# Fourteen gate/up units as 7-product 2x2 blocks, with sums of the down operand on GpSimd

## The chip, the cores and the metric

The kernel runs on one core of one Trainium2 chip. The metric is the device time of one execution in microseconds (us), lower is better. The kernel before takes 265.61 us (median of 20 runs, 265.26 to 267.59).

## The reference, cut to what matters

Two blocks work on 2048 tokens with 640 features, and a sigmoid gate mixes them. Only the second block is touched by the change, except that its down projection is summed with the first block's output projection in one product.

```python
def _B_ref(x, w_gate, w_up, w_down):             # 640 -> 1728 -> 640
    return (_gelu(x @ w_gate) * (x @ w_up)) @ w_down
...
g = _sigmoid((x * gate_w).sum(-1, keepdims=True))
a = _A_ref(x, A_wqkv, A_wo)                      # linear attention
return g * a + (1 - g) * b
```

## The kernel before

The tokens go in four quarters of 512. For each quarter, a *gate/up stage* (13 full f tiles of 128 and one half tile) makes the hidden `hT`; a *down stage* for the previous quarter follows. The order is E(1), down(0), E(2), down(1), E(3), down(2), down(3). An f tile of gate/up is ten matmuls of 512 columns, one gelu on ScalarE and one multiplication on VectorE:

```python
def e_mm(ps, w, ft, q, t0=0, tw=QW):                      # QW = 512, ND = 5
    for dk in range(ND):
        nc.tensor.matmul(ps[:, t0 : t0 + tw], lhsT=w[:, dk, ft * P : (ft + 1) * P],
                         rhs=xT[q][:, dk, t0 : t0 + tw], start=(dk == 0), stop=(dk == ND - 1))

def e_out(q, ft, psg, psu):
    gl = work.tile([P, QW], BF16, name="gl")
    nc.scalar.activation(out=gl[:], in_=psg[:], func=ACT.Gelu_apprx_tanh)
    nc.vector.scalar_tensor_tensor(out=hT_cur[q][:, ft, :], in0=psu[:], scalar=HS, in1=gl[:],
                                   op0=ALU.mult, op1=ALU.mult)
```

Down is already done with 7 instead of 8 products of 2x2 blocks. That needs sums of its first operand over k tiles in three parts: h (6 tiles of `hT`), p (2 tiles of the attention operand `pqT`), x (one mixed tile). Each part has four sums, per half `a` of the tokens, all on VectorE, all with two operands in SBUF:

```python
def phase_S(q, part, a=None):
    ...
    sums(s3, blk(0, 0), blk(1, 0), ALU.subtract)
    sums(s1, blk(1, 0), blk(1, 1), ALU.add)
    sums(s2, s1, blk(0, 0), ALU.subtract)
    sums(s4, blk(0, 1), s2, ALU.subtract)
```

The down stage runs seven products for each half. An accumulator bank `x` is used three times, with a copy by ScalarE (`keep`) between; VectorE joins (`join`). A dictionary says what is queued beside which unit or product ("F": before the first product, "D": behind the first join).

```python
product(x, a, 0, 0, 0, 0, 0, 0, True, True)
c1 = keep("c1", x, 0)                       # ScalarE; product 3 below writes x again
...
product(x, a, 2, 0, 0, 2, 0, 0, False, True)      # product 3, needs c1 done
...
join(d[:], b22, 0, c2)                      # VectorE
beside("D", q, a)
...
(2, 2): [(s_tiles, 1), (phase_S, 1, "h", 0)],     # gate/up stage 2, third unit
(2, 3): [(phase_S, 1, "h", 1)],
(2, 4): [(phase_S, 1, "p"), (phase_S, 1, "x")],
```

Apart from set-up, GpSimd only forms products for the denominators of the attention (`den_mul`, `den_out`).

## Time and profile before

| | before |
|---|---|
| time, median of 20 | 265.61 us |
| span of the profiled run | 264.8 us |
| gate/up stage 2 / down(1) / gate/up 3 / down(2) and (3) | 29.14 / 17.87 / 29.14 / 35.90 us |

The stage lengths here and below are my differences between the starts of first matmuls in the timeline of TensorE; the last one runs to the end of the last matmul.

These are three lines of the page of the kernel before: the busy times of the engines, and the chain that ended last, by engine and by line (L186 is the gate/up matmul, L603 the down matmul).

```profile
PE 258.1 (97%) x1569; PEld 145.0 (55%) x1587; DVE 185.1 (70%) x343; ACT 94.5 (36%) x187; POOL 50.2 (19%) x50
...
PE 93%; DMA 4%; issue 0%; DVE 0%; SPq 0%
PE banks L186 44%; PE banks L603 26%; PE banks L249 14%; PE banks L347 6%; DMA wqk<-in_A_wqkv_dram 3%; PE banks L338 2%; DMA x_all<-in_A_x_dram 1%; PE banks L610 1%; PE banks L478 0%; PE banks L447 0%; DVE o_out L629 0%; SPq L122 0%; PE banks L417 0%
```

TensorE is the bound. The timeline of TensorE gives the price of a unit: start, duration, what, count. The first two lines are the same five matmuls, 1.08 us apart; the last three are the turn from the second to the third product of down(1), without a gap.

```profile
150.18 1.24 PE L186 MATMUL banks<-xT_87,wu 128*128 128x512 bf16 x5
151.26 1.24 PE L186 MATMUL banks<-xT_87,wg 128*128 128x512 bf16 x5
...
179.33 1.11 PE L603 MATMUL banks<-wd,hb 128*128 128x320 bf16 x7
180.28 0.57 PE L603 MATMUL banks<-m_all,pqT_1489 128*128 128x320 bf16 x3
180.68 1.39 PE L603 MATMUL banks<-t_1098,s_2_1578 128*128 128x320 f16 x9
```

The timeline of VectorE in gate/up stage 2 (first fence) has the same sums twice, once while GpSimd works (second fence, the timeline of GpSimd) and once while it rests.

```profile
156.46 1.13 DVE L61 TENSOR_TENSOR sw<-hb 128x768 f16<-128x768 bf16 x1
157.51 1.76 DVE L61 TENSOR_TENSOR s_1_1577<-hb 128x768 f16<-128x768 bf16 x1
...
162.05 0.55 DVE L61 TENSOR_TENSOR sw<-hb 128x768 f16<-128x768 bf16 x1
162.52 0.55 DVE L61 TENSOR_TENSOR s_1_1577<-hb 128x768 f16<-128x768 bf16 x1
```

```profile
154.67 2.50 POOL L533 TENSOR_TENSOR pq_90<-pq_90,rg 128x640 bf16<-128x640 bf16 x2 [2.39 <-DVE rg L524]
157.13 3.40 POOL L510 TENSOR_TENSOR prod<-pq_91,zrep 128x640 f32<-128x640 bf16 x2
```

The same sum takes 0.55 us alone and 1.13 or 1.76 us beside a GpSimd operation. The profile before shows no wait of TensorE in the gate/up and down stages.

### The profile page before, as it was taken

How to read it: one execution, taken by the hardware profiler on the slowest of the kernel's cores; microseconds unless marked ns; L12 is line 12 of the kernel's file. 1: busy time of each engine (PE TensorE's matmuls, PEld its weight loads, DVE VectorE, ACT ScalarE, POOL GpSimd, SP SyncE). 2: the span in 40 equal slices, each digit the busy share in tenths (PEclk: the TensorE clock that was granted, in tenths of full speed). 3: DMA queues.
4: the chain of work that ended last, by engine and by line, in shares of the span. 5: the costliest groups of instructions: out<-in, count | busy, mean ns of one | idle time of the engine just before them, and what ended most of it. 6: DMA issues, size and time to landing. Idle time of an engine off the chain costs nothing.

```text
span 264.8 us, 4162 instructions
## 1 busy us (share of the span) xinstructions
PE 258.1 (97%) x1569; PEld 145.0 (55%) x1587; DVE 185.1 (70%) x343; ACT 94.5 (36%) x187; POOL 50.2 (19%) x50
## 2 busy tenths in 40 slices
PE   8799999999999999999999999999999999999994
PEld 4454444555556775444566544447664444767672
DVE  0765348598889995699994889982335997676132
ACT  3679222655455333832231122223112222312110
POOL 5000000000000003685000762383001820000000
PEclk9999999999999999999999999999999999999999
DMA  7899999000000009125001050022110220011011
GB/s 225 259 285 313 213 321 246 1 0 2 0 0 2 0 16 332 51 59 118 0 0 52 0 136 15 0 54 50 50 50 2 50 50 0 2 50 36 17 50 50
DMA packets 34959, 20.91 MB, mean 79 GB/s; under 512 B 20732, under 2 KB 34940, under 8 KB 34940
## 3 DMA queue, kind: packets, MB, share of 16 engines
q1 hardware_dynamic: 34498, 20.16, 27.8%
q10 hardware_dynamic: 442, 0.49, 0.6%
q8 instruction: 12, 0.20, 0.3%
q14 instruction: 7, 0.06, 0.1%
HBM read 12.62 MB, written 2.62 MB: 58 GB/s over the span
## 4 chain that ended last, share of the span: by engine, by line
PE 93%; DMA 4%; issue 0%; DVE 0%; SPq 0%
PE banks L186 44%; PE banks L603 26%; PE banks L249 14%; PE banks L347 6%; DMA wqk<-in_A_wqkv_dram 3%; PE banks L338 2%; DMA x_all<-in_A_x_dram 1%; PE banks L610 1%; PE banks L478 0%; PE banks L447 0%; DVE o_out L629 0%; SPq L122 0%; PE banks L417 0%
## 5 line engine op out<-in xcount | busy, mean ns | idle before, releaser
L191 ACT ACTIVATE gl<-banks 128x512 bf16<-128x512 f32 x52 | 31.0, 598 | 74.6 <-PE banks L186 70.6
L186 PEld LDWEIGHTS <-wu 128*128 128x128 bf16 x260 | 25.5, 98 | 30.6
L186 PEld LDWEIGHTS <-wg 128*128 128x128 bf16 x260 | 25.2, 98 | 29.3 <-issue 0.5
L192 DVE SCALAR_TENSOR_TENSOR hT_148<-banks,gl 128x512 bf16<-128x512 f32 x26 | 17.4, 682 | 12.7 <-PE banks L186 10.8
L192 DVE SCALAR_TENSOR_TENSOR hb<-banks,gl 128x512 bf16<-128x512 f32 x26 | 17.4, 677 | 10.9 <-PE banks L186 8.7
L266 ACT ACTIVATE phi<-banks 128x512 bf16<-128x512 f32 (+1 forms) x36 | 18.7, 526 | 15.5 <-ACT eneg L267 6.3
L510 POOL TENSOR_TENSOR prod<-pq_89,zrep 128x640 f32<-128x640 bf16 x2 | 2.8, 1406 | 96.2 <-ACT zrep L418 96.2
L625 ACT ACTIVATE m_all<-banks,omg_s 128x320 f32<-128x320 f32 x16 | 8.4, 527 | 27.2 <-PE banks L603 27.2
L629 DVE SCALAR_TENSOR_TENSOR o_out<-banks,omg_s,m_all 128x320 bf16<-128x320 f32 x24 | 12.2, 541 | 5.9 <-PE banks L603 5.9
L186 PE MATMUL banks<-xT_85,wu 128*128 128x512 bf16 x65 | 16.1, 379 | 0.0
L186 PE MATMUL banks<-xT_87,wu 128*128 128x512 bf16 x65 | 16.1, 379 | 0.0
L186 PE MATMUL banks<-xT_88,wu 128*128 128x512 bf16 x65 | 16.1, 379 | 0.0
L186 PE MATMUL banks<-xT_86,wu 128*128 128x512 bf16 x63 | 16.0, 379 | 0.1
L186 PE MATMUL banks<-xT_85,wg 128*128 128x512 bf16 x63 | 16.0, 379 | 0.1
L186 PE MATMUL banks<-xT_87,wg 128*128 128x512 bf16 x62 | 16.0, 379 | 0.2
L186 PE MATMUL banks<-xT_88,wg 128*128 128x512 bf16 x62 | 16.0, 379 | 0.2
L186 PE MATMUL banks<-xT_86,wg 128*128 128x512 bf16 x63 | 15.7, 379 | 0.1
L629 DVE SCALAR_TENSOR_TENSOR m_all<-banks,omg_s,m_all 128x320 f32<-128x320 f32 x8 | 4.4, 551 | 14.6 <-PE banks L603 14.5
L249 PE MATMUL banks<-wqk,xT_85 128*128 128x512 bf16 (+2 forms) x78 | 12.4, 302 | 1.4 <-DMA wqk<-in_A_wqkv_dram 1.3
L510 POOL TENSOR_TENSOR prod<-pq_90,zrep 128x640 f32<-128x640 bf16 x4 | 7.4, 1866 | 24.4 <-DVE den L516 24.4
L629 DVE SCALAR_TENSOR_TENSOR o_out<-banks,omg_s,sw 128x320 bf16<-128x320 f32 x8 | 4.4, 549 | 10.7 <-PE banks L603 5.6
L625 ACT ACTIVATE sw<-banks,omg_s 128x320 f32<-128x320 f32 x8 | 4.2, 527 | 20.6 <-PE banks L603 20.6
(216 smaller groups left out, 469.9 us busy)
## 6 DMA issues: line engine op xcount, KB each, us to landing
out_dram<-o_out SPq DMA_DIRECT2D x16, 160.0 KB, 1.8
wd<-in_B_w_down_dram SPq DMA_DIRECT2D x1, 2080.0 KB
x_all<-in_A_x_dram SPq DMA_DIRECT2D x3, 640.0 KB, 6.2
wqk<-in_A_wqkv_dram SPq DMA_DIRECT2D x1, 800.0 KB
wg<-in_B_w_gate_dram SPq DMA_DIRECT2D x1, 800.0 KB, 8.2
wu<-in_B_w_up_dram SPq DMA_DIRECT2D x1, 800.0 KB
wv<-in_A_wqkv_dram SPq DMA_DIRECT2D x1, 800.0 KB
wo_g<-in_A_wo_dram SPq DMA_DIRECT2D x2, 375.0 KB
```

The lines of the kernel that those rows point to most:

```text
L186: nc.tensor.matmul(ps[:, t0 : t0 + tw], lhsT=w[:, dk, ft * P : (ft + 1) * P], rhs=xT[q][:, dk, t0 : t0 + tw], start=(dk == 0), stop=(dk == ...
L191: nc.scalar.activation(out=gl[:], in_=psg[:], func=ACT.Gelu_apprx_tanh)
L192: nc.vector.scalar_tensor_tensor(out=hT_cur[q][:, ft, :], in0=psu[:], scalar=HS, in1=gl[:], op0=ALU.mult, op1=ALU.mult)
L249: nc.tensor.matmul(ps[:, 0 : hi - lo], lhsT=xT[q][:, dk, sl * P : (sl + 1) * P], rhs=wqk[:, dk, lo:hi], start=(dk == 0), stop=(dk == ND - 1),)
L266: nc.scalar.activation(out=e[:, lo:top], in_=ps[:, lo:top], func=ACT.Exp)
L338: nc.tensor.matmul(gp[:, 0:HALF], lhsT=x_all[:, st, (ND - 1) * P : ND * P], rhs=pk[st][:, j * HALF : (j + 1) * HALF], start=(st == 0), sto ...
L347: nc.tensor.matmul(bank[:, 0:HALF], lhsT=lhsT, rhs=rhs, start=(start and n == 0), stop=(stop and n == NG2 - 1), skip_group_check=True)
L510: nc.gpsimd.tensor_tensor(out=prod[:], in0=pq[st][:], in1=zrep[:], op=ALU.mult)
L603: nc.tensor.matmul(bank[:, 0:HALF], lhsT=lhs(sa, ia, ka * KS + kk, a), rhs=rhs(sb, kb * KS + kk, jb), start=(start and kk == 0), stop=(sto ...
L610: nc.tensor.matmul(bank[:, 0:HALF], lhsT=lhsT, rhs=wd[r : r + FL, NF - 1, j * HALF : (j + 1) * HALF], start=st_, stop=not a, skip_group_ch ...
L625: nc.scalar.activation(out=c[:], in_=bank[:, 0:HALF], func=ACT.Copy, scale=omg[i])
L629: nc.vector.scalar_tensor_tensor(out=out, in0=bank[:, 0:HALF], scalar=omg[i], in1=c[:], op0=ALU.mult, op1=ALU.add)
```

## The change

The intent is to save TensorE time. In gate/up stages 2 and 3, seven of the fourteen units become 2x2 blocks, gate and up by token halves, over four of the five k tiles: one matmul of 512 columns and sixteen of 256 instead of ten of 512. The price is sums of weights (formed once on GpSimd, written out to memory, fetched back a piece per unit), sums of tokens, and a longer evacuation: two accumulator copies and one scaled copy on ScalarE, three VectorE operations, and the final multiplication on GpSimd. To make room on VectorE, the h sums of the first token half go to GpSimd, one at a time, in the slots of the ordinary units between (in quarter 3 one sum of the second half too; nine in all). The core of the diff:

```diff
+    def phase_EW(q, ft, early):
+        ...
+        ew_mm(ub, 1, wt(wu, 4), xt(4, slice(0, QW)), True)
+        ew_mm(ub[:, lo_h], 2, wt(wu, 2), t_(4))
+        ew_mm(gb[:, lo_h], 1, wt(wg, 4), xt(4, lo_h), True)
+        ew_mm(gb[:, hi_h], 1, s_(5), xt(4, hi_h))
+        ew_mm(x[:, lo_h], 2, s_(2), t_(2), False, True)
+        nc.scalar.copy(out=cg[:, hi_h], in_=x[:, lo_h])
+        early()
+        ew_mm(gb[:, lo_h], 2, wt(wg, 2), xt(2, lo_h))
+        ew_mm(ub[:, hi_h], 2, s_(1), t_(1), False, True)
+        ew_mm(gb[:, hi_h], 2, s_(4), xt(2, hi_h), False, True)
+        ew_mm(x[:, lo_h], 2, s_(3), t_(3), False, True)
+        ...
+        nc.vector.tensor_tensor(out=cg[:, hi_h], in0=ub[:, hi_h], in1=cg[:, hi_h], op=ALU.add)
+        nc.scalar.activation(out=ut[:, 1], in_=x[:, lo_h], func=ACT.Copy, scale=HS)
+        ew_finish()                                  # gelu and product of the unit before
+        nc.vector.tensor_tensor(out=cg, in0=gb, in1=cg, op=ALU.add)
+        nc.vector.scalar_tensor_tensor(out=ut[:], in0=ub..., scalar=HS, in1=ut[:, 1:2]..., op0=ALU.mult, op1=ALU.add)
+        def finish():
+            nc.scalar.activation(out=gl[:], in_=cg, func=ACT.Gelu_apprx_tanh)
+            nc.gpsimd.tensor_tensor(out=hT_cur[q][:, ft, :], in0=ut[:]..., in1=gl[:], op=ALU.mult)
...
+    def pool_S(q, a, *which):
+        phase_S(q, "h", a, which, nc.gpsimd)
...
-        (2, 2): [(s_tiles, 1), (phase_S, 1, "h", 0)],
-        (2, 3): [(phase_S, 1, "h", 1)],
-        (2, 4): [(phase_S, 1, "p"), (phase_S, 1, "x")],
...
+        (2, 2): [(pool_S, 1, 0, 3)],
+        (2, 5): [(pool_S, 1, 0, 1), (phase_S, 1, "p", 0, (3, 1))],
+        (2, 8): [(pool_S, 1, 0, 2), (phase_S, 1, "p", 0, (2, 4))],
+        (2, 11): [(pool_S, 1, 0, 4), (phase_S, 1, "x", 0)],
+        (2, 13): [(den_mul, 10, 11)],
+        ("F", 1, 0): [(phase_S, 1, "h", 1), (phase_S, 1, "p", 1), (phase_S, 1, "x", 1)],
...
+        2: [0, 1, 2, -4, -5, 3, -6, -7, 12, -8, -9, 11, -10, 13],     # negative: a new unit
```

The cuts ("...") hide the tiles, the weight sums and the slots of quarter 3, which are like those of quarter 2 but for the down stage, where only three h sums stand before the first product and p and x stand behind the first join.

More of the change, by code (lines that the diff above doesn't have):

```diff
@@ L67 @@
     work = ctx.enter_context(tc.tile_pool(name="work", bufs=3))
+    dram = ctx.enter_context(tc.tile_pool(name="dram", bufs=1, space=bass.MemoryType.DRAM))
     psum = ctx.enter_context(tc.tile_pool(name="psum", bufs=1, space=bass.MemoryType.PSUM))
@@ L89, with pk_tiles @@
     x_sb = [x_all[:, 4 * q : 4 * q + 4, :] for q in range(NQ)]
-    pk_q = [ov.tile([P, 4, D], BF16, name=f"pk{q}", tag="slab_a", bufs=NQ) for q in range(NQ)]
-    pk = [pk_q[t // 4][:, t % 4, :] for t in range(NT)]
+    WF = tuple(range(4, 12))
+    WS = 2 * 4 + 1
+    ws = [ov.tile([P, 2, WS, P], FP16, name=f"ws{i}", tag="slab_a", bufs=NQ) for i in range(3)]
+    ws.append(ov.tile([P, 2, WS, P], FP16, name="ws3", tag="slab_g"))
+    pk_q = []
+    pk = {}
+    def pk_tiles(qs):
+        for q in qs:
+            pk_q.append(ov.tile([P, 4, D], BF16, name=f"pk{q}", tag="slab_a", bufs=NQ))
+            for t in range(4):
+                pk[4 * q + t] = pk_q[q][:, t, :]
+    pk_tiles((0,))
     WQK = 2 * D + 1
@@ L193, in e_out, with phase_E @@
                                        op0=ALU.mult, op1=ALU.mult)
-    def phase_E(q, ft):
+    def phase_E(q, ft, early=None):
         if ft < NF - 1:
@@ L198, in phase_E @@
             e_mm(psg, wg, ft, q)
+            if early:
+                early()
+                ew_finish()
             psu = ps_tile("ps_u")
@@ L204, in phase_E @@
             e_mm(pgu, wgu, 0, q)
+            if early:
+                early()
+                ew_finish()
             gl = work.tile([P, QW], BF16, name="gl")
@@ L208, in phase_E, with w_sums @@
                                            in1=gl[0:FL, :], op0=ALU.mult, op1=ALU.mult)
+    stash = dram.tile([len(WF), P, WS, P], FP16, name="stash")
+    def w_sums(i):
+        f0 = WF[2 * i] * P
+        g, u = (w[:, :, f0 : f0 + 2 * P].rearrange("p k (f c) -> p f k c", f=2) for w in (wg, wu))
+        o = ws[i]
+        s1, s2, s3, s4 = (o[:, :, 2 * n : 2 * n + 2, :] for n in range(4))
+        for out, a0, a1, op in ((s1, u[:, :, 0:2, :], u[:, :, 2:4, :], ALU.add), (s2, s1, g[:, :, 0:2, :], ALU.subtract),
+                                (s3, g[:, :, 0:2, :], u[:, :, 0:2, :], ALU.subtract),
+                                (s4, g[:, :, 2:4, :], s2, ALU.subtract),
+                                (o[:, :, 8:9, :], g[:, :, 4:5, :], u[:, :, 4:5, :], ALU.subtract)):
+            nc.gpsimd.tensor_tensor(out=out, in0=a0, in1=a1, op=op)
@@ new lines, in w_stash, with x_tiles, t_sums, blk @@
+    def w_stash(i):
+        for f in range(2):
+            dma(out=stash[2 * i + f], in_=ws[i][:, f])
+    HT = QW // 2
+    ew = {}
+    def x_tiles():
+        tx = big.tile([P, 4, 2, HT], FP16, name="tx", tag="pq", bufs=NQ)
+        ew["tx"] = [tx[:, n] for n in range(4)]
+    def t_sums(q):
+        def blk(k, j):
+            return xT[q][:, 2 * k : 2 * k + 2, j * HT : (j + 1) * HT]
+        t1, t2, t3, t4 = ew["tx"]
+        for out, a0, a1 in ((t1, blk(0, 1), blk(0, 0)), (t2, blk(1, 1), t1), (t3, blk(1, 1), blk(0, 1)),
+                            (t4, blk(1, 0), t2)):
+            sums(out, a0, a1, ALU.subtract)
@@ new lines, in ew_tiles, with w_fetch @@
+    def ew_tiles():
+        cg = big.tile([P, 2, QW], FP32, name="cg", tag="pq", bufs=NQ)
+        ew["cg"] = [cg[:, 0], cg[:, 1], zacc[:, 0:QW]]
+        ew["n"] = 0
+        ew["first"] = {}
+        ew["open"] = []
+    def w_fetch(*keys, eng=dma):
+        if "ring" not in ew:
+            wr = big.tile([P, 2, WS, P], FP16, name="wr", tag="xT", bufs=NQ - 1)
+            ew["ring"] = [wr[:, 0], wr[:, 1]]
+            ew["m"] = 0
+            ew["at"] = {}
+        for q, ft in keys:
+            slot = ew["ring"][ew["m"] % 2]
+            ew["m"] += 1
+            eng(out=slot, in_=stash[WF.index(ft)])
+            ew["at"][q, ft] = slot
@@ new lines, in ew_finish, with ew_mm, ew_first @@
+    def ew_finish():
+        for f in ew.get("open", ()):
+            f()
+        ew["open"] = []
+    lo_h, hi_h = slice(0, HT), slice(HT, QW)
+    def ew_mm(out, k, lhs, rhs, start=False, stop=False):
+        for n in range(k):
+            nc.tensor.matmul(out, lhsT=lhs(n), rhs=rhs(n), start=start and n == 0, stop=stop and n == k - 1,
+                             skip_group_check=True)
+    def ew_first(q, ft):
+        x = ps_tile("ps_wx")
+        cg = ew["cg"][ew["n"] % 3]
+        ew["n"] += 1
+        ew_mm(x[:, lo_h], 2, lambda n: wg[:, n, ft * P : (ft + 1) * P], lambda n: xT[q][:, n, lo_h], True, True)
+        nc.scalar.copy(out=cg[:, lo_h], in_=x[:, lo_h])
+        ew["first"][q, ft] = x, cg
@@ new lines, in phase_EW, with wt, xt, s_ @@
+    def phase_EW(q, ft, early):
+        fs = slice(ft * P, (ft + 1) * P)
+        sw_ = ew["at"][q, ft]
+        if (q, ft) not in ew["first"]:
+            ew_first(q, ft)
+        x, cg = ew["first"][q, ft]
+        def wt(w, k0):
+            return lambda n: w[:, k0 + n, fs]
+        def xt(k0, c):
+            return lambda n: xT[q][:, k0 + n, c]
+        def s_(i):
+            return lambda n: sw_[:, 2 * (i - 1) + n, :]
+        def t_(i):
+            return lambda n: ew["tx"][i - 1][:, n, :]
+        ub, gb = ps_tile("ps_wu"), ps_tile("ps_wg")
+        ew_mm(ub, 1, wt(wu, 4), xt(4, slice(0, QW)), True)
[4 more added lines that the diff above has]
+        nc.scalar.copy(out=cg[:, hi_h], in_=x[:, lo_h])
+        early()
+        ew_mm(gb[:, lo_h], 2, wt(wg, 2), xt(2, lo_h))
+        ew_mm(ub[:, hi_h], 2, s_(1), t_(1), False, True)
+        ew_mm(gb[:, hi_h], 2, s_(4), xt(2, hi_h), False, True)
+        ew_mm(x[:, lo_h], 2, s_(3), t_(3), False, True)
+        ut = work.tile([P, 2, HT], FP32, name="ut", tag="prod", bufs=2)
+        nc.vector.tensor_tensor(out=cg[:, hi_h], in0=ub[:, hi_h], in1=cg[:, hi_h], op=ALU.add)
+        nc.scalar.activation(out=ut[:, 1], in_=x[:, lo_h], func=ACT.Copy, scale=HS)
+        ew_finish()
+        nc.vector.tensor_tensor(out=cg, in0=gb, in1=cg, op=ALU.add)
+        nc.vector.scalar_tensor_tensor(out=ut[:], in0=ub.rearrange("p (j c) -> p j c", j=2), scalar=HS,
+                                       in1=ut[:, 1:2].to_broadcast([P, 2, HT]), op0=ALU.mult, op1=ALU.add)
+        def finish():
+            gl = work.tile([P, QW], BF16, name="gl")
+            nc.scalar.activation(out=gl[:], in_=cg, func=ACT.Gelu_apprx_tanh)
+            nc.gpsimd.tensor_tensor(out=hT_cur[q][:, ft, :], in0=ut[:].rearrange("p j c -> p (j c)"), in1=gl[:],
+                                    op=ALU.mult)
+        ew["open"].append(finish)
@@ L305, in k_first @@
         held.clear()
-    g_sb = ov.tile([P, ND, D], BF16, name="g_sb", tag="slab_g")
     def x_blk(i, k):
@@ L561, with phase_S @@
     TW = 2 * P
-    def phase_S(q, part, a=None):
+    def phase_S(q, part, a=None, which=(3, 1, 2, 4), eng=nc.vector):
         lo, hi = PART[part]
@@ L568, in blk @@
             return ktiles(part, k, hT_cur[q], pqT[q])[:, :, i * TW + c0 : i * TW + c1]
-        s1, s2, s3, s4 = (SS[q, i][:, lo:hi, c0:c1] for i in range(1, 5))
-        sums(s3, blk(0, 0), blk(1, 0), ALU.subtract)
-        sums(s1, blk(1, 0), blk(1, 1), ALU.add)
-        sums(s2, s1, blk(0, 0), ALU.subtract)
-        sums(s4, blk(0, 1), s2, ALU.subtract)
+        s = {i: SS[q, i][:, lo:hi, c0:c1] for i in range(1, 5)}
+        for i in which:
+            a0, a1, op = {3: (blk(0, 0), blk(1, 0), ALU.subtract), 1: (blk(1, 0), blk(1, 1), ALU.add),
+                          2: (s[1], blk(0, 0), ALU.subtract), 4: (blk(0, 1), s[2], ALU.subtract)}[i]
+            eng.tensor_tensor(out=s[i], in0=a0, in1=a1, op=op)
+    def pool_S(q, a, *which):
+        phase_S(q, "h", a, which, nc.gpsimd)
     side = {}
@@ L681 @@
             phase_E(0, ft)
+            if ft == 5:
+                for i in range(len(ws)):
+                    w_sums(i)
             if ft in (8, 9, 10, 11):
                 x_sums((3, 1, 2, 4)[ft - 8])
+        for i in range(len(ws)):
+            w_stash(i)
+        pk_tiles((1, 2, 3))
+        g_sb = ov.tile([P, ND, D], BF16, name="g_sb", tag="slab_g")
         g4 = [banks[:, b * QW : (b + 1) * QW] for b in (6, 7)]
@@ L743 @@
         (1, 11): [(phase_S, 0, "x", 0)],
-        ("F", 0, 0): [(phase_S, 0, "h", 1)],
+        (1, 12): [(den_mul, 4, 5)],
+        ("F", 0, 0): [(w_fetch, (2, 4), (2, 5)), (phase_S, 0, "h", 1)],
         ("D", 0, 0): [(phase_S, 0, "p", 1), (phase_S, 0, "x", 1)],
-        ("F", 0, 1): [(den_mul, 4, 5)],
-        ("D", 0, 1): [(den_inv, 4), (den_mul, 6, 7), (den_out, 4, 5)],
-        (2, 0): [(den_inv, 6), (den_out, 6, 7)],
-        (2, 2): [(s_tiles, 1), (phase_S, 1, "h", 0)],
-        (2, 3): [(phase_S, 1, "h", 1)],
@@ L751 @@
-        (2, 4): [(phase_S, 1, "p"), (phase_S, 1, "x")],
-        (2, 5): [(den_mul, 8, 9)],
-        (2, 7): [(den_inv, 8), (den_mul, 10, 11), (den_out, 8, 9)],
-        (2, 9): [(den_inv, 10), (den_out, 10, 11)],
-        (3, 0): [(den_mul, 12, 13)],
-        (3, 2): [(den_inv, 12), (den_mul, 14, 15), (den_out, 12, 13)],
-        (3, 4): [(den_inv, 14), (den_out, 14, 15)],
-        (3, 5): [(s_tiles, 2), (phase_S, 2, "h", 0)],
-        (3, 6): [(phase_S, 2, "h", 1)],
-        (3, 7): [(phase_S, 2, "p"), (phase_S, 2, "x")],
@@ L761 @@
-        ("F", 2, 0): [(s_tiles, 3), (phase_S, 3, "h", 0)],
-        ("D", 2, 0): [(phase_S, 3, "p", 0)],
-        ("F", 2, 1): [(phase_S, 3, "x", 0), (phase_S, 3, "h", 1)],
-        ("D", 2, 1): [(phase_S, 3, "p", 1)],
-        ("F", 3, 0): [(phase_S, 3, "x", 1)],
-    })
+        ("F", 0, 1): [(den_inv, 4), (den_mul, 6, 7), (den_out, 4, 5)],
+        ("D", 0, 1): [(den_inv, 6), (den_out, 6, 7), (x_tiles,)],
+        (2, 0): [(t_sums, 2), (ew_tiles,), (s_tiles, 1), (den_mul, 8, 9)],
+        (2, 1): [(den_inv, 8), (den_out, 8, 9)],
@@ new lines @@
+        (2, 2): [(pool_S, 1, 0, 3)],
[4 more added lines that the diff above has]
+        ("F", 1, 0): [(phase_S, 1, "h", 1), (phase_S, 1, "p", 1), (phase_S, 1, "x", 1)],
+        ("F", 1, 1): [(den_inv, 10), (den_mul, 12, 13), (den_out, 10, 11)],
+        ("D", 1, 1): [(den_inv, 12), (den_mul, 14, 15), (den_out, 12, 13)],
@@ new lines @@
+        (3, 0): [(t_sums, 3), (s_tiles, 2)],
+        (3, 1): [(den_inv, 14), (den_out, 14, 15)],
+        (3, 2): [(pool_S, 2, 0, 3)],
+        (3, 5): [(pool_S, 2, 0, 1), (phase_S, 2, "p", 0, (3, 1))],
+        (3, 8): [(pool_S, 2, 0, 2), (phase_S, 2, "p", 0, (2, 4))],
+        (3, 11): [(pool_S, 2, 0, 4), (phase_S, 2, "x", 0)],
+        (3, 13): [(pool_S, 2, 1, 3)],
+        ("F", 2, 0): [(phase_S, 2, "h", 1, (1, 2, 4))],
+        ("D", 2, 0): [(phase_S, 2, "p", 1), (phase_S, 2, "x", 1), (s_tiles, 3)],
@@ L767 @@
+        ("F", 2, 1): [(phase_S, 3, "h", 0)],
+        ("D", 2, 1): [(phase_S, 3, "p", 0), (phase_S, 3, "x", 0)],
+        ("F", 3, 0): [(phase_S, 3, "h", 1)],
+        ("D", 3, 0): [(phase_S, 3, "p", 1), (phase_S, 3, "x", 1)],
+    })
+    runs = {
+        1: list(range(1, NF)),
+        2: [0, 1, 2, -4, -5, 3, -6, -7, 12, -8, -9, 11, -10, 13],
+        3: [0, 1, 2, -4, -5, 3, -6, -7, 12, -8, -9, 11, -10, 13],
+    }
+    wins = [(q, -ft) for q in runs for ft in runs[q] if ft < 0]
     with tc.manual_schedule():
@@ L768 @@
         for q in range(1, NQ):
-            for ft in range(q == 1, NF):
-                phase_E(q, ft)
-                beside(q, ft)
+            for n, ft in enumerate(runs[q]):
+                nxt = runs[q][n + 1] if n + 1 < len(runs[q]) else 0
+                early = (lambda f=-nxt: ew_first(q, f)) if nxt < 0 else (lambda: None)
+                if ft < 0:
+                    phase_EW(q, -ft, early)
+                    k = wins.index((q, -ft)) + 2
+                    if k < len(wins):
+                        w_fetch(wins[k], eng=dma2)
+                else:
+                    phase_E(q, ft, early if q > 1 else None)
+                beside(q, n + (q == 1))
@@ L772 @@
+            ew_finish()
             phase_F(q - 1)
```

## The prediction

> **What bounds it now.** TensorE. The engine summary shows matmuls busy 258.1 of 264.8 us (97%), VectorE 70%, ScalarE 36%, GpSimd 19%. The chain of waits is 93% TensorE (gate/up line 43.9%, down 26.0%); the rest is the first loads (about 4%). From 15 us on, the table by stretches has TensorE full everywhere.
>
> **What the change removes.** The timeline shows 5 matmuls of 512 columns every 1.079 us: 215.8 ns each, 2.158 us for a unit of 10. In the q/k stage 15 matmuls take 2.71 us, 10 of 512 and 5 of 257 columns, so 257 columns cost (2.71-2.158)/5 = 110 ns. Both agree with the Trainium skill, "TensorE: Matmul & The Clock Gate", Back-to-back issue gap: N/2.4 + 2.5 ns when warm. A new unit has one 512 and sixteen 256 matmuls: 215.8 + 16 x 109.2 = 1.963 us (estimate). That saves 0.195 us a unit, 14 units: 2.7 us. The weight load hides behind 257 columns, so behind 256.
>
> **What it adds.** Per new unit (estimates from neighbouring sizes in the groups): VectorE 0.43 + 0.65 + 0.69 = 1.77 us instead of 0.69; ScalarE three 256-wide moves of 0.38 and a gelu of 0.6 instead of one gelu; GpSimd a 512 product, about 1.1 us. Token sums 4 x 0.41 us per quarter on VectorE. Weight sums on GpSimd, 20 operations, about 20 us, between roughly 20 and 45 us, then 2.4 MB out and, a piece per unit, back. Operand sums of down go to GpSimd (about 1.6 us each). Totals: VectorE 185 to about 195 us, ScalarE to about 110, GpSimd to about 100.
>
> **Critical path.** All hidden, I expect. In a pair of new units VectorE needs 1.77 of 1.96 us and recovers in the ordinary unit between; two new units and one ordinary one take exactly the 8 banks, so a bank has about 6 us to come free. The accumulator that is copied between its products has about 0.5 to 0.9 us for a 0.38 us copy: tight, but enough. A weight piece has about 4 us to land, for 2 to 3. Small losses expected: (a) weight sums on GpSimd against the x sums and the q/k stage on VectorE. The trace shows 768-wide sums at 0.55 us alone and 1.13 to 1.76 us while GpSimd runs, as the skill's "SBUF — State Buffer", Who interferes with whom, says of two-input VectorE work. The q/k stage has only about 0.5 us slack for its banks, but VectorE has about 3 us idle before it; (b) the start of each changed quarter, where token sums and denominators make VectorE late by under 1 us. I allow 0.3 us.
>
> **Predicted: 263.2 us (0.9% less), range 262.4 to 265.2.** Faster by over 2%: 2%; within 2%: 94%; slower by over 2%: 4%.
>
> **What would show it.** New units 1.96 us apart; TensorE busy about 255.5 us; no TensorE waits on ScalarE or VectorE in the changed quarters over 0.1 us; down and q/k stages unchanged (18.1 us a quarter; 2.98 us a step). Weight sums over by about 45 us, the stash landed before the second k group is written (about 52 us).
>
> **What would make it wrong.** 256-column matmuls slower than 110 ns in long rows; the accumulator copies coming late in every unit (0.1 us each costs 1.4 us in all); GpSimd slower than estimated, stalling the q/k stage through its buffers; weight pieces landing late. A gain over 2.8 us has no source.

## The result, and the profile after

The changed kernel is correct and takes 270.12 us (median of 10 runs, 269.03 to 271.83), against 265.61 us. The ratio is 1.0168 (95% interval 1.0142 to 1.0193). Ratios are the mean time of one kernel's fast runs over that of the other's of the same rounds, so not quite the ratio of the medians quoted. It is slower by 1.7%, where 0.9% less was predicted.

The lines of the page after that answer to those above, busy times and chain by engine (in the lines below, L199 and L290 are the gate/up matmuls, L743 and L750 the down matmuls):

```profile
PE 257.4 (96%) x1665; PEld 154.9 (58%) x1685; DVE 208.5 (78%) x386; ACT 108.2 (40%) x229; POOL 103.7 (39%) x93
...
PE 80%; DVE 11%; issue 3%; ACT 2%; DMA 2%; SPq 0%; DVEq 0%; ACTq 0%
```

TensorE was on the chain for 93% and is for 80%; VectorE, off it before, has 11%. The stages say where (us):

| | gate/up 2 | down(1) | gate/up 3 | down(2), (3) |
|---|---|---|---|---|
| before | 29.14 | 17.87 | 29.14 | 35.90 |
| after | 28.20 | 23.69 | 28.15 | 37.60 |
| difference | -0.94 | +5.82 | -0.99 | +1.70 |

Everything from the first gate/up unit to the start of gate/up 2 takes 133.56 us in both traces, so the weight sums, their way out to memory and back, and the q/k stage cost nothing. The gate/up stages did get shorter. The down stages, which run the same matmuls as before, got longer. The waits in the profile after (who waited for whom: us in total, times, longest us) name it.

```profile
ACT gl L342 <- DVE cg L336: 8.6, 7, 3.0
...
PE banks L743 <- ACT sw L765: 3.1, 2, 1.5
...
PE banks L750 <- DVE m_all L769: 2.3, 1, 2.3
```

In the timeline of TensorE the first two lines are the starts of two new units, 1.97 us apart; the rest is down(1). The third product starts 1.53 us late; the half tiles stop for 2.27 us; and the six matmuls behind them take 1.48 us, where six such took 0.98 before.

```profile
154.36 0.38 PE L290 MATMUL banks<-xT_90,wu 128*128 128x512 bf16 x1
...
156.33 0.38 PE L290 MATMUL banks<-xT_90,wu 128*128 128x512 bf16 x1
...
177.91 0.57 PE L743 MATMUL banks<-m_all,pqT_1485 128*128 128x320 bf16 x3
180.01 1.38 PE L743 MATMUL banks<-t_1133,s_2_1596 128*128 128x320 f16 x9 [1.53 <-ACT sw L765]
...
187.57 0.43 PE L750 MATMUL banks<-wd,hb 64*128 64x320 bf16 x3 [2.27 <-DVE m_all L769]
...
188.09 1.48 PE L743 MATMUL banks<-hb 128*128 128x320 f16 x6
```

Why was ScalarE late with the copy `c1` (tile sw, L765)? Its timeline shows it stuck in order behind the gelu of the last new unit, which waited 3.00 us for VectorE:

```profile
178.44 0.63 ACT L342 ACTIVATE gl<-cg 128x512 bf16<-128x512 f32 x1 [3.00 <-DVE cg L336]
178.98 0.57 ACT L225 ACTIVATE gl<-banks 64x512 bf16<-64x512 f32 x1
179.45 0.51 ACT L765 ACTIVATE sw<-banks,omg_s 128x320 f32<-128x320 f32 x1
```

And VectorE's timeline shows what made it late, with GpSimd's behind it for the same time:

```profile
160.19 0.68 DVE L337 SCALAR_TENSOR_TENSOR ut<-banks,ut 128x512 f32<-128x512 f32 x1
...
162.12 0.28 DVE L711 TENSOR_TENSOR sw<-pqT_1485 128x256 f16<-128x256 bf16 x1
162.32 1.24 DVE L711 TENSOR_TENSOR s_1_1595<-pqT_1485 128x256 f16<-128x256 bf16 x1
...
168.27 0.28 DVE L711 TENSOR_TENSOR s_2_1596<-s_1_1595,pqT_1485 128x256 f16<-128x256 f16 x1
168.59 1.61 DVE L711 TENSOR_TENSOR sp<-pqT_1485,s_2_1596 128x256 f16<-128x256 bf16 x1
...
174.30 0.69 DVE L205 SCALAR_TENSOR_TENSOR hT_151<-banks,gl 128x512 bf16<-128x512 f32 x1 [0.65 <-ACT gl L204]
174.90 0.22 DVE L711 TENSOR_TENSOR sw<-hb 128x128 f16<-128x128 bf16 x1
175.03 1.66 DVE L711 TENSOR_TENSOR s_1_1595<-hb,pqT_1485 128x128 f16<-128x128 bf16 x1
...
177.65 0.69 DVE L336 TENSOR_TENSOR cg<-banks,cg 128x512 f32<-128x512 f32 x1
```

```profile
159.48 1.64 POOL L711 TENSOR_TENSOR sw<-hb 128x768 f16<-128x768 bf16 x1
161.08 2.34 POOL L343 TENSOR_TENSOR hT_151<-ut,gl 128x512 bf16<-128x512 f32 x2
163.38 1.69 POOL L711 TENSOR_TENSOR s_1_1595<-hb 128x768 f16<-128x768 bf16 x1
...
168.34 1.71 POOL L711 TENSOR_TENSOR s_2_1596<-s_1_1595,hb 128x768 f16<-128x768 f16 x1
...
174.97 1.65 POOL L711 TENSOR_TENSOR sp<-hb,s_2_1596 128x768 f16<-128x768 bf16 x1
```

A sum of 128 columns that takes 0.22 us began just after a GpSimd sum and ended with it, 1.66 us later. The change itself arranges this: it puts the GpSimd sum and the VectorE sums of p or x in the same slot. The sum at 162.32 is the exception: it meets the final products of two new units (L343, from 161.08), which the change moved to GpSimd too, and ends 0.14 us after them. The VectorE operation with only one SBUF operand, at 160.19, takes its usual 0.68 us in the middle of a GpSimd sum.

The clock has a part too. The table by half-microsecond stretches (columns: stretch; its length; busy time of TensorE, weight loads, VectorE, ScalarE, GpSimd with counts; granted TensorE clock; DMA share; GB/s) shows it at half speed behind the 2.27 us gap:

```profile
187.50:188.00 0.50, 0.42 (x6) 0.22 (x5) 0.50 (x3) 0.00 (x0) 0.00 (x0) 1.00 0.00 0
...
188.50:189.00 0.50, 0.50 (x4) 0.30 (x2) 0.40 (x1) 0.00 (x0) 0.00 (x0) 0.50 0.00 0
...
192.00:192.50 0.50, 0.50 (x6) 0.35 (x5) 0.47 (x2) 0.08 (x1) 0.50 (x1) 1.00 0.62 213
```

The trace's clock record has one stretch of 3.41 us at 0.5 within the span; half of it is lost, 1.71 us. Of the 11 runs of the changed kernel (the profiled one too), 6 have a mean clock of 0.994 and take 271.12 us in the mean, 5 have 1.000 and take 269.37: 1.75 us less. The profiled run is one of the former. So down(1)'s 5.82 us are 1.53 + 2.27 of waits, 1.71 of half clock, and 0.31 of small gaps.

### The profile page after: what moved, and what is told of

It is laid out like the page before. It is cut to its first block, busy times and chain, and to the rows that moved or that the text cites. A ratio compares the mean times of both kernels' runs of the same rounds, so it can differ in the third digit from the quotient of the medians.

```text
span 268.7 us, 4575 instructions
## 1 busy us (share of the span) xinstructions
PE 257.4 (96%) x1665; PEld 154.9 (58%) x1685; DVE 208.5 (78%) x386; ACT 108.2 (40%) x229; POOL 103.7 (39%) x93
## 4 chain that ended last, share of the span: by engine, by line
PE 80%; DVE 11%; issue 3%; ACT 2%; DMA 2%; SPq 0%; DVEq 0%; ACTq 0%
PE banks L199 28%; PE banks L743 23%; PE banks L387 16%; PE banks L484 6%; PE banks L290 4%; PE banks L475 2%; DMA wqk<-in_A_wqkv_dram 2%; DVE cg L336 1%; DVE s_1_1595 L711 1%; DVE ut L337 1%; DVE cg L333 1%; ACT gl L342 1%; PE banks L750 1%; DVE sw L711 1%; DVE hT_151 L205 1%
## 5 line engine op out<-in xcount | busy, mean ns | idle before, releaser
L204 ACT ACTIVATE gl<-banks 128x512 bf16<-128x512 f32 x38 | 22.6, 597 | 40.1 <-PE banks L199 36.9
L199 PEld LDWEIGHTS <-wu 128*128 128x128 bf16 x190 | 18.6, 98 | 20.7
L199 PEld LDWEIGHTS <-wg 128*128 128x128 bf16 x190 | 18.3, 98 | 19.8 <-issue 0.5
L205 DVE SCALAR_TENSOR_TENSOR hb<-banks,gl 128x512 bf16<-128x512 f32 x19 | 12.9, 677 | 8.4 <-ACT gl L204 4.7
L765 ACT ACTIVATE m_all<-banks,omg_s 128x320 f32<-128x320 f32 x16 | 8.4, 527 | 25.7 <-PE banks L743 25.7
L290 PE MATMUL banks<-tx,wr 128*128 128x256 f16 x84 | 16.0, 272 | 0.5 <-ACT cg L326 0.5
L199 PE MATMUL banks<-xT_88,wu 128*128 128x512 bf16 x65 | 16.1, 379 | 0.0
L199 PE MATMUL banks<-xT_89,wu 128*128 128x512 bf16 x63 | 16.0, 379 | 0.1
L199 PE MATMUL banks<-xT_88,wg 128*128 128x512 bf16 x63 | 16.0, 379 | 0.1
L199 PE MATMUL banks<-xT_89,wg 128*128 128x512 bf16 x63 | 15.7, 379 | 0.1
L765 ACT ACTIVATE sw<-banks,omg_s 128x320 f32<-128x320 f32 x8 | 4.2, 523 | 23.5 <-PE banks L743 23.5
L290 PEld LDWEIGHTS <-wr 128*128 128x128 f16 x126 | 12.3, 98 | 2.3 <-issue 0.9
L387 PE MATMUL banks<-wqk,xT_91 128*128 128x512 bf16 (+1 forms) x59 | 11.4, 343 | 0.1
L387 PE MATMUL banks<-wqk,xT_89 128*128 128x512 bf16 (+1 forms) x58 | 11.4, 342 | 0.1
L387 PE MATMUL banks<-wqk,xT_90 128*128 128x512 bf16 (+1 forms) x59 | 11.4, 343 | 0.1
L343 POOL TENSOR_TENSOR hb<-ut,gl 128x512 bf16<-128x512 f32 x7 | 8.1, 1159 | 7.8 <-ACT gl L342 7.8
```

The source lines that it names most:

```text
L290: nc.tensor.matmul(out, lhsT=lhs(n), rhs=rhs(n), start=start and n == 0, stop=stop and n == k - 1, skip_group_check=True)
L343: nc.gpsimd.tensor_tensor(out=hT_cur[q][:, ft, :], in0=ut[:].rearrange("p j c -> p (j c)"), in1=gl[:], op=ALU.mult)
L387: nc.tensor.matmul(ps[:, 0 : hi - lo], lhsT=xT[q][:, dk, sl * P : (sl + 1) * P], rhs=wqk[:, dk, lo:hi], start=(dk == 0), stop=(dk == ND - 1),)
L765: nc.scalar.activation(out=c[:], in_=bank[:, 0:HALF], func=ACT.Copy, scale=omg[i])
```

## The experiments

Theory A: collisions. A VectorE sum with two SBUF operands stands still until a running GpSimd operation that reads SBUF is done; in the changed stages this makes VectorE late, ScalarE waits for it in order, and TensorE waits for ScalarE. Rival B: VectorE simply has too much work. Rival C: the place of the second-half sums, all three parts ahead of the first join in down(1). "The changed kernel" below is the kernel after; each edit is against it.

The table gathers the results. Stages are of the profiled run, in us.

| kernel | median us | ratio to before (95%) | gate/up 2 | down(1) | gate/up 3 | down(2),(3) |
|---|---|---|---|---|---|---|
| changed | 270.12 | 1.0168 (1.0142-1.0193) | 28.20 | 23.69 | 28.15 | 37.60 |
| v1_px_pool | 265.77 | 1.0009 (0.9957-1.0061) | 27.77 | 20.41 | 27.77 | 36.02 |
| v2_h_dve | 265.68 | 1.0017 (0.9967-1.0068) | 28.65 | 20.53 | 27.77 | 35.98 |
| v3_px_after | 268.15 | 1.0093 (1.0070-1.0117) | 28.19 | 20.73 | 28.87 | 37.61 |
| v4_later | 265.25 | 0.9990 (0.9955-1.0025) | 27.77 | 19.76 | 27.77 | 36.60 |
| w1_later_after | 264.23 | 0.9951 (0.9934-0.9968) | 27.77 | 18.47 | 27.77 | 36.59 |
| w2_pool_after | 263.59 | 0.9938 (0.9919-0.9957) | 27.76 | 19.13 | 27.77 | 35.90 |
| w3_gate | 265.14 | 0.9990 (0.9974-1.0006) | 27.77 | 19.77 | 27.77 | 36.59 |
| w4_memset (wrong result) | 265.29 | 0.9989 (0.9964-1.0015) | 27.77 | 21.60 | 27.77 | 35.90 |
| y1_x_early | 264.25 | 0.9926 (0.9892-0.9960) | 28.39 | 18.23 | 27.76 | 35.91 |
| y2_hdiff | 263.59 | 0.9899 (0.9869-0.9929) | slow profile, not used | | | |

### v2_h_dve: the h sums back on VectorE

```diff
     def pool_S(q, a, *which):
-        phase_S(q, "h", a, which, nc.gpsimd)
+        phase_S(q, "h", a, which, nc.vector)
```

> The h sums that the change moved to GpSimd go back to VectorE, at the same places; GpSimd keeps the final products and the denominators. VectorE gets about 2.25 us more work a quarter (four sums of 0.55 us) but the three sums a quarter that met a 1.65 us GpSimd sum no longer do. Theory A: less late by about 1.5 us a quarter, so faster than the changed kernel: 266.5 to 269. Rival B: later by 2.25 us a quarter: slower than 270.1, 271 to 274. Rival C: about 270, unchanged.

Measured: 265.68 us, 4.4 us below the changed kernel, with more work on VectorE. It is even better than theory A had it (266.5 to 269). Rival B expected 271 or more and falls: giving VectorE four more sums of 0.55 us a quarter made the kernel faster. Moving the h sums away was what hurt. Between full-clock runs the gain is 3.8 us (265.56 in the mean of three, against 269.37). In its profile both 1.53 us waits are gone, and the 2.27 us wait before the half tiles is not. (The expectation is wrong in one point: in quarter 2 only two of the three sums had met an h sum, as shown above.)

### w4_memset: GpSimd equally busy, but reading nothing

```diff
     def pool_S(q, a, *which):
-        phase_S(q, "h", a, which, nc.gpsimd)
+        for i in which:
+            for _ in range(2):
+                nc.gpsimd.memset(SS[q, i][:, 0:KH, a * P : a * P + P], 0.0)
```

> Wrong results on purpose. The changed kernel, with every h sum on GpSimd replaced by two fills of the same tile, which read nothing. If the collision is one of reading (VectorE operations with two SBUF operands against GpSimd operations that read SBUF), the VectorE sums in the same slot take 0.22 to 0.42 us beside the fills, and the time falls to 265 to 267.5. If any GpSimd work holds such sums up, they still take as long as the fills run (over 0.7 us), and the time stays above 268.

The result is wrong. Measured: 265.29 us. Order and slots are those of the changed kernel, and the pair of fills takes 1.53 us where the sum took 1.64 to 1.71. First the timeline of VectorE, then that of GpSimd:

```profile
162.49 1.26 DVE L711 TENSOR_TENSOR sw<-pqT 128x256 f16<-128x256 bf16 x1
...
168.66 0.28 DVE L711 TENSOR_TENSOR s<-s,pqT 128x256 f16<-128x256 f16 x1
168.97 0.29 DVE L711 TENSOR_TENSOR sp<-pqT,s 128x256 f16<-128x256 bf16 x1
...
174.19 0.22 DVE L711 TENSOR_TENSOR sw<-hb 128x128 f16<-128x128 bf16 x1
174.33 0.22 DVE L711 TENSOR_TENSOR s<-hb,pqT 128x128 f16<-128x128 bf16 x1
```

```profile
161.33 2.27 POOL L343 TENSOR_TENSOR hT<-ut,gl 128x512 bf16<-128x512 f32 x2
...
168.71 1.53 POOL L716 MEMSET s<- 128x768 f16 x2
...
174.24 1.53 POOL L716 MEMSET sp<- 128x768 f16 x2
```

Beside a fill the sums take their 0.22 to 0.29 us. The one that meets a GpSimd multiplication, at 162.49, still takes 1.26. So it is not GpSimd's activity but its reading that holds the sums up. The Trainium skill, "SBUF — State Buffer", section Who interferes with whom, says just this: a VectorE instruction with two SBUF inputs contends with a GpSimd instruction that reads SBUF, "not with one that only writes it". This trace agrees in both halves. Taking the collisions with these nine GpSimd sums away is worth 4.5 us between full-clock runs (264.89 in the mean of three, against 269.37), and 4.8 between the medians.

What is left in this profile is in down(1), 21.60 us: a wait of 1.88 us before the half tiles and, behind it, again a stretch of 3.41 us at half clock (1.71 us lost). The wait, in the timeline of TensorE:

```profile
185.43 0.43 PE L752 MATMUL banks<-wd,hb 64*128 64x320 bf16 x3 [1.88 <-DVE m_all L771]
```

The half clock runs from 186.83 to 190.24 by the trace's clock record.

### v4_later: the same sums on the same engines, one unit later

```diff
-        (2, 5): [(pool_S, 1, 0, 1), (phase_S, 1, "p", 0, (3, 1))],
+        (2, 5): [(pool_S, 1, 0, 1)],
+        (2, 6): [(phase_S, 1, "p", 0, (3, 1))],
 ...                                  # the same for (2, 8), (2, 11), and for quarter 3
```

> Same work on the same engines; the VectorE sums of the pq and mixed tiles come one unit later than the GpSimd sums of the same quarter, not in the same slot. Theory A: the collisions with the 1.65 us GpSimd sums mostly vanish (each 0.3 to 0.6 us instead of 1.2 to 1.7), TensorE waits shrink, 265.5 to 268.5. Rival B: the work is the same, so about 270, unchanged. Rival C: about 270, unchanged.

Measured: 265.25 us, 4.9 us below the changed kernel. The gate/up stages come to 27.77 us, and the 1.53 us waits are gone in both quarters. It does not separate the theories as cleanly as I meant: in quarter 2 the p sums lose 0.83 us instead of 2.29, but the x sums still lose 2.0 us, only now behind the evacuation of the last new unit instead of ahead of it. Part of the gain is thus that what is late is no longer on the way to the accumulator copy.

### v1_px_pool: the p and x sums on GpSimd too

```diff
-        (2, 5): [(pool_S, 1, 0, 1), (phase_S, 1, "p", 0, (3, 1))],
+        (2, 5): [(pool_S, 1, 0, 1), (phase_S, 1, "p", 0, (3, 1), nc.gpsimd)],
 ...                                  # the same for (2, 8), (2, 11), and for quarter 3
```

> All first-half-token sums of the down operand (the pq and mixed k tiles too) on GpSimd in both changed quarters; the changed kernel otherwise. Theory A (collisions): VectorE sums of two SBUF operands stand still until a running GpSimd operation ends; three such sums a quarter took 1.2 to 1.7 us instead of 0.22 to 0.28, 3.7 us lost in quarter 2 and 4.2 in quarter 3, and this lateness stops TensorE at the start of down. It predicts that the waits of 1.5 us before the third product of down go away in both quarters, and 265 to 267 us. Rival B (VectorE simply has too much work in a changed quarter): only about 2 us of work a quarter goes away; waits shrink but stay, 267 to 269. Rival C (the sums set ahead of the join in the down stage of quarter 1): the 2.3 us wait there and the lowered clock stay, 268 to 269.

Measured: 265.77 us, as theory A had it. Both 1.5 us waits are gone. The wait before the half tiles in down(1) is still there, 2.4 us, and 2 of the 4 runs show a clock of 0.992 or 0.994. So C is a second cause beside A.

### v3_px_after: second-half p and x sums behind the first join in down(1)

```diff
-        ("F", 1, 0): [(phase_S, 1, "h", 1), (phase_S, 1, "p", 1), (phase_S, 1, "x", 1)],
+        ("F", 1, 0): [(phase_S, 1, "h", 1)],
+        ("D", 1, 0): [(phase_S, 1, "p", 1), (phase_S, 1, "x", 1)],
```

> Only the order in the down stage of quarter 1: the second-half pq and mixed sums stand behind the first join, as they do in quarter 0, instead of ahead of it. Theory C: the 2.3 us wait before the half tiles goes (the join comes about 2 us earlier), the clock stays up, 265.5 to 267.5. Theories A and B: that wait goes but VectorE stays about 4 us late there and the two waits of 1.5 us before the third product stay: 267.5 to 269, and the runs of lower clock become rare.

Measured: 268.15 us, 268.03 to 268.59, within what A and B expected. The 2.3 us wait shrinks to 0.4, and all four runs are at full clock; the two 1.5 us waits stay. C alone therefore explains 2.0 us between the medians, or 1.1 us between the means of full-clock runs (268.23 against 269.37), and not the rest.

### w1_later_after and w2_pool_after: both repairs

The edits are v4 with v3, and v1 with v3.

> Both repairs together: the VectorE sums one unit later than the GpSimd sums, and in the down stage of quarter 1 the second-half pq and mixed sums behind the first join. If the two causes are collisions and the place of those sums, nothing is left of the waits: gate/up stages of 27.8 us and down stages of 17.9 us in the trace, 262.9 to 263.6 us, 0.8 to 1% below the kernel before; all runs at full clock. If something else holds TensorE up (the accumulator copies, the fetched weights), over 264.3.

> All first-half sums on GpSimd and the second-half pq and mixed sums behind the first join. Same expectation as the other repair, 262.9 to 263.8 us; slightly later if GpSimd, now the busier, still meets the VectorE sums at the start of down.

Measured: 264.23 and 263.59 us. Both beat the kernel before (by 0.5 and 0.6%), and w2 is within what was expected, but w1 is not: something was left. The stage table says where. In w1, down(1) is still 0.60 us and the last two down stages 0.69 us too long. The waits name ScalarE's second copy, 0.8 us in both together: it stands in order behind a copy of the last gate/up half tile, which VectorE evacuates behind two x sums that took 1.14 and 1.33 us instead of 0.22. In w2, down(1) is 1.26 us too long, with waits of 0.5 and 0.4 us on joins: there the first sums of down on VectorE (1.13, 1.68 and 1.76 us) meet GpSimd's last final product and the denominators' products behind it.

### w3_gate: the denominators' products held back

```diff
-        (2, 13): [(den_mul, 10, 11)],
-        ("F", 1, 0): [(phase_S, 1, "h", 1)],                     # as in w1
+        ("F", 1, 0): [(phase_S, 1, "h", 1, (3, 1, 2)), (pool_S, 1, 1, 4), (den_mul, 10, 11)],
```

> The first repair, and the denominators' products of quarter 2 on GpSimd held back behind one sum that needs VectorE, so that they no longer meet the first sums of down. If those collisions (the first sums of down took 1.1 to 1.8 us instead of 0.55) still cost TensorE time, 0.3 us or more below the first repair; if they are only in slack, the same within 0.2 us.

Measured: 265.14 us, 0.9 us *above* w1; neither expectation holds. The h sums now take 0.55 us each, but the products moved onto the p sums behind the join, which took 1.12, 1.49 and 1.38 us instead of 0.28, and TensorE waited 1.7 us for a join after them. A collision was not removed, only moved to a place where it costs more.

### y1_x_early and y2_hdiff: the remaining collisions moved into idle time

y1 is w1 with the first-half x sums on GpSimd in the second slot of each changed stage, where it is idle:

```diff
-        (2, 1): [(den_inv, 8), (den_out, 8, 9)],
+        (2, 1): [(phase_S, 1, "x", 0, (3, 1, 2, 4), nc.gpsimd), (den_inv, 8), (den_out, 8, 9)],
 ...
-        (2, 12): [(phase_S, 1, "x", 0)],                         # as in w1
```

y2 is y1 with the difference for the half tile, which stood at the head of down and took 1.44 us instead of 0.22 there, formed in slot 9 of the gate/up stage.

> The first repair (VectorE pq sums one unit later, second-half sums behind the first join), and the four first-half mixed sums on GpSimd in the second slot of each changed quarter, where GpSimd stands idle for 4 us, instead of on VectorE one unit before down, where two of the four took 1.1 to 1.6 us and delayed the last gate/up tile and with it the accumulator copy that TensorE waited 0.3 and 0.5 us for. By the stage lengths of the trace that repair still lost 0.6 us in the down stage of quarter 1 and 0.7 us after: if that is the cause, both go and the time is 263.0 to 263.8 us. If VectorE, now earlier, meets the denominators' products on GpSimd instead, the wait before the half tiles in quarter 1 comes back (0.5 us or more) and 263.6 to 264.3 comes out.

> The same, and the small difference of the half tile, which took 1.1 us instead of 0.22 at the head of down, is formed in the middle of the quarter. Takes up to 0.9 us from what VectorE does ahead of the first join: if a wait before the half tiles is there in the other run, it goes, 262.8 to 263.6 us. No difference if there is no such wait.

y1 gave 264.25 us (263.06 to 265.44). That lies in the range of the second branch of what was expected, but not for its reason: the wait before the half tiles is not in the profile. Its down stages are nearly whole (18.23 and 35.91 us), but in its profile gate/up 2 is 28.39 us, where the weight loads waited 0.7 us for one fetched piece. That late piece is in this one profile; whether it is in the other runs is open.

y2 gave 263.59 us over all six runs, one of which (the profiled one) was slow at 302.5 us. The five fast runs are 262.78 to 263.82 us, mean 263.37, ratio 0.9899: 1.0% below the kernel before. In those rounds the kernel before took 266.17 us in the mean, in those of w1 and w2 265.49; against the latter the lead would be 0.8%. Its profile can't be used for stages. Like w1, w2 and y1, this version beats both kernels. That it is better than y1 is not shown (the intervals overlap); y1 had no wait before the half tiles, so no difference was expected.

## Why the prediction was wrong

**Right: the matmul arithmetic.** Predicted 1.963 us for a new unit; 1.97 us apart in the trace. A changed stage without waits should be 7 x 1.963 + 6 x 2.158 + 1.079 = 27.77 us; it is 27.77 in v1, v4, w1, w3 and w4. Twice 29.14 - 27.77 is 2.74 us, the 2.7 us predicted. The formula of the Trainium skill ("TensorE: Matmul & The Clock Gate", Back-to-back issue gap), N/2.4 + 2.5 ns, held: 215.8 ns for 512 columns, and by these 27.77 us 109.2 ns for 256, with a new weight each. The section gives the formula for an isolated matmul and about 131 ns for 512 columns in a stream of weight loads and matmuls; the 215.8 ns of this stream contradict that figure. TensorE's busy time came to 257.4 us, above the 255.5 predicted, but that contains the half-clock stretch.

**Right: what costs nothing.** Weight sums, stash and q/k stage: 133.56 us before and after. ScalarE 108 us (predicted 110) and GpSimd 104 (100).

**Wrong: "All hidden, I expect. In a pair of new units VectorE needs 1.77 of 1.96 us and recovers in the ordinary unit between".** The prediction knew of the collision: its point (a) gave the numbers, 0.55 us alone and 1.13 to 1.76 us beside GpSimd. It applied them to the weight sums, where nothing came of them, and not to the sums that stand beside the work that the change moves to GpSimd. Their excess over the 0.28 and 0.22 us alone, read off the trace, is 0.96 (beside the final products) + 1.33 + 1.44 (beside h sums in the same slot) = 3.7 us in quarter 2. At the head of down(1) the half tile's difference (1.44 us instead of 0.22) and the first h sum (1.68 instead of 0.55) meet GpSimd products as well, 2.35 us more. VectorE's total is 208.5 us, not 195. Nor does it recover in the ordinary unit: it idles 0.65 us there, because the multiplication waits for a gelu that stands on ScalarE behind the gelu of the last new unit, which itself waits for VectorE. That the collisions are the main cause is shown by w4 (fills instead of sums, 4.5 us faster at full clock) and v2 (more work, 3.8 us faster).

**Wrong: "down and q/k stages unchanged".** I held the banks to be the place where lateness would show, saw 6 us of slack there, and stopped. The lateness showed one stage on: through ScalarE's order into the accumulator copy of down (1.53 us in each of two down stages), and through VectorE's order into the first join of down(1), where the change had put all second-half sums ahead of it (2.27 us), the p and x sums among them with 2 us. v3 shows the second, v1, v2, v4 and w4 the first.

**Not foreseen: the clock.** Behind the 2.27 us gap the profiled run has half clock, and 6 of 11 runs have a mean clock of 0.994 and are 1.75 us longer. It goes with the gap: w4's profile has the same stretch behind 1.88 us, and the 32 runs of v3, v4, w1, w2, w3 and y1, whose profiles show no gap above 1.74 us there, have no clock under 0.997. But a gap of that size does not always bring it: the profiles of v1 and v2 have gaps of 2.37 and 2.27 us and no such stretch. The prediction had none of it.

**The sum.** Against 2.74 us gained stand, in the profiled run, 0.43 + 0.38 us of small waits in the gate/up stages, 5.82 in down(1) and 1.70 in the last two: 8.33 lost, so 5.59 us longer between the two profiles from gate/up 2 on, or 3.88 without the half clock. The full-clock runs differ by 269.37 - 265.85 (mean of before) = 3.5 us. The 0.3 us allowed for losses was the wrong term: 8.33 us were lost, 6.62 without the clock. With more of the collisions moved out of the way (y2) the mean is 263.37 us, near the 263.2 predicted for the change as it stood. That does not confirm the number: the sums are placed otherwise, and no usable profile shows which waits are left.

## What to carry to other kernels

Moving work to an idle GpSimd is not free for VectorE: before doing so, lay both engines' orders side by side, and price each two-operand SBUF sum on VectorE at the rest of the GpSimd operation that it meets, if that one reads SBUF, above all where the change itself queues both in the same slot. When an engine off the critical path becomes late, follow the lateness through every in-order queue into the next stage, not only through the buffers of its own. And when a gap of some 2 us opens on TensorE, look at the clock behind it: it may cost nearly as much again (here 1.71 us behind gaps of 2.27 and 1.88 us, though not in every run).

## What the Trainium skill lacked or had wrong

- "TensorE: Matmul & The Clock Gate", Why this matters for your kernels, asks for no idle gaps above about 3 us. Here one gap of 2.27 us was followed by 3.41 us at half clock in the profiled run, and 6 of 11 runs of that kernel had a mean clock of 0.994, in the mean 1.75 us longer. In w4's profile a gap of 1.88 us was enough for the same 3.41 us. The same kernel with the gap cut to 0.4 us (v3) had none in 4 runs. Gaps of 2.37 and 2.27 us in the profiles of v1 and v2 were not followed by it; what decides it, no run here shows.
- "SBUF — State Buffer", Who interferes with whom, was right, and its exception for a GpSimd instruction that only writes as well (0.22 to 0.29 us beside fills). It gives no durations for short sums: a 128-column sum of 0.22 us took 1.66 us, seven and a half times as long.
- No page that I read works out the in-order consequence that made this matter: a late VectorE, a gelu on ScalarE waiting 3.00 us for it, and a 0.5 us copy queued behind that gelu stopping TensorE for 1.53 us.
